# Step 0's last head pair in two halves of two batches, fewer key rows, and a new order of the opening, in a gated linear attention with a feed-forward on one core

## The chip, the cores and the metric

One core of one Trainium2 chip runs the whole kernel. The metric is the time of one execution in microseconds of device time, the median of the runs shown. The engines are called by their names in the profile: PE is TensorE, DVE is VectorE, ACT is ScalarE, POOL is GpSimd, SP is the queue that issues most loads.

## The reference, cut to what matters

```
f = 1 / (1 + exp(-f_logit))                      # batch 4, 8 heads, 768 tokens, 48 channels
for t in range(768):
    state = f[t] * state + k[t] (outer) v[t]     # per batch and head, 48 x 48
    y[t] = q[t] @ state
h = x @ w_in                                     # x: y as 3072 tokens x 384;  w_in 384 x 2048
g = h if h >= 1, 0 if h <= -1, else (h + 1)**2 / 4
out = g @ w_out                                  # 2048 x 384
```

## The kernel before, in words

The 768 tokens are cut into six steps of 128. The eight heads go two by two: four pairs, numbered 0 to 3, each on 2 x 48 partitions, with four batches of 128 tokens side by side (512 columns). Pair 3's rows are split over the three 128-row blocks of x from step 1 on; in step 0 pair 3 stands in rows of its own.

Step 0 is the opening, and it has functions of its own. For each pair `first_loads` loads 192 KB of logits (`raw<-in_l`, for pair 2 `sd<-in_l`) and 512 KB of keys and queries (`kq<-in_k`), and ACT takes the logarithm of the gates in two passes, "log" (L455, L456). `first_gates` sums the logarithms by eight PE matmuls with a triangular mask (L465; each batch is a matmul), takes two exponentials on ACT, "sig" (L468, L469), and multiplies keys and queries by them on DVE, "gate" (L473, L474). `scores` (L572) makes the attention scores of the pair, 16 PE matmuls of 48 rows, and `masks` (L585) multiplies them by the mask on DVE. `last_heads` and `half_tile(own)` (L806) multiply scores by values, `half_tile(not own)` (L836) adds pair 3's result to blocks 0 to 2 of x, and whichever of the two comes first for a block begins its sum; where `own` comes first, a matmul with zeros clears the bank first (L827). The result is split into a high and a low part (L660 on ACT, L661 on DVE), and `unit_0` (L860) begins the feed-forward.

The feed-forward is 96 units, 16 to a step (L266 makes h, nine matmuls of 512 columns; L269, L272, L277 the activation on ACT and DVE; L889 and L280 its high and low part; L287 the product with w_out, nine matmuls). Its weights come as 32 pieces of 384 KB (`raw<-in_w`), and each is split by ACT and DVE (L367, L369, L372, L373) in the first hundred microseconds, while units already run.

The attention of steps 1 to 5 is put between units by hand. `TURNS` says after which unit's in-products pair n (n counts pairs over steps: 4 to 7 are step 1) has its keys turned: on PE for step 1 (L640), on DVE later (L655). `VISITS` gives for pairs n and n+1 the three units at which scores are made (L621), at which the first products with values and the states are made (L688, L759), and at which the outputs follow (L710). The gates of steps 1 to 5 need a scan on DVE (L503), two exponentials on ACT and two products on DVE (L508, L509), and six small moves by SP for pair 3 (`kq<-kq`, L296). `START` is the order in which the opening's work is given to PE, and `WARM` is a row of matmuls on zeros (L337) that PE runs first.

PE runs in the order in which the program gives its work. For DVE, ACT, POOL and SP a planner (`Plan.order`) places each instruction at the time it works out from a table of costs: among those that are ready it takes the one whose latest allowed time, counted back from the end through all that depends on it, is first. Where PE would wait in the plan, it fills the place with matmuls on zeros (L332).

Of the kernel before, what the change touches and what calls it, by code (L numbers as in the profile page):

```python
# [18 lines left out]
AF = mybir.ActivationFunctionType  # L19
ALU = mybir.AluOpType  # L20
PSUM = bass.MemoryType.PSUM

B, H, S, D = 4, 8, 768, 48
C = 128
NI = S // C
NP = H // 2
R = 112
DM, DF = H * D, 2048
NJ = DF // 128
N = B * C  # L30
# [15 lines left out]
NG = (NP + (NI - 1) * NT) * B  # L46


SMALL_PRODUCTS = ("gates", "scores", "heads", "own", "tile", "both", "begin", "before", "part", "states", "parts", "half", "turn")

HOP, LANDING, PER_KB, NEAR, ADDING, PATIENCE, FLAG_BY = 200, 2200, 3.0, 3500, 1500, 0, 60000
COST = dict(gates=870, log=500, mm=227, scores=1100, heads=950, own=1200, tile=680, both=1090, begin=480, before=930, part=560, states=850, parts=830, turn=350, first=110, last=95,
            rows=316, scan=1140, dve=602, small=200, half=490, sums=467, gate=600, act=575, bits=520, join=465, part_hi=440, cast_384=330, cast=400, round=485, copy=520, turned=412, sig=538, decay=226,
            issue=480, near=600, least=300)


TURNS = {4: 4, 5: 5, 6: 9, 7: 9, 8: 19, 9: 19, 10: 25, 11: 25, 12: 28, 13: 28, 14: 37, 15: 37, 16: 40, 17: 40, 18: 47, 19: 47, 20: 61, 21: 61, 22: 70, 23: 70}
VISITS = {4: (5, 6, 7), 6: (10, 12, 13), 8: (21, 22, 25), 10: (25, 26, 28), 12: (28, 32, 37), 14: (37, 39, 40), 16: (40, 46, 47), 18: (47, 60, 61), 20: (61, 69, 70), 22: (70, 75, 77)}
START = (("gates", 3), ("gates", 0), ("scores", 3), ("mask", 3), ("gates", 1), ("scores", 0), ("mask", 0), ("gates", 2), ("last", 3),
         ("scores", 1), ("mask", 1), ("heads", 0), ("scores", 2), ("mask", 2), ("tile", 2), ("tile", 1), ("tile", 0), ("heads", 1), ("heads", 2), ("unit", 0), ("unit", 1), ("unit", 2))  # L60
WARM = 28 * (128,) + 4 * (256,)
BY_PRODUCT, ON_EITHER = (), 16
AFTER = {0: (("turn", 0), ("turn", 1)), 1: (("states", 0),), 2: (("turn", 2), ("turn", 3)), 3: (("states", 2),)}

# [119 lines left out]
def gla_moe(ctx: ExitStack, tc: tile.TileContext, ff, ld, kd, kqd, f0, vv, vl, wd, maskd, identd, gates, values, headsd, out):  # L184
# [50 lines left out]
    def wide(a):  # L235
        return a.rearrange("r b c -> r (b c)")
# [197 lines left out]
    def spread(a):  # L434

        return of_heads(a)[..., 0:D]
# [7 lines left out]
    def first_loads(n):  # L444

        c, a = att[n], LOGS[n]
        if n == NP - 1:
            ready["mask"] = add("ACT", "issue", lambda: nc.scalar.dma_start(mask_z, maskd[:, 0:C + 1]), kb=64)
            ready["sel"] = dma(ident, identd, 64)
        raw_l = WEIGHTS[n][1][:, 0:BOTH]  # L450
        l = dma(raw_l, ld[n], 192)
        rows = 128
        c["lk"] = dma(kq[n][:rows, 0:2 * N], kd[n, :rows], 4 * rows)

        e = sca("log", lambda: nc.scalar.activation(spread(a), raw_l.rearrange("t (m h d) -> t m h d", m=B, h=2), AF.Exp, scale=-1.0), l, cleared)  # L455
        c["l"] = sca("log", lambda: nc.scalar.activation(spread(a), spread(a), AF.Ln, bias=one), e, set_consts)  # L456

    def first_gates(n):

        t, c, (kw, qw) = kq[n][:R], att[n], [a[:R] for a in WEIGHTS[n]]  # L460
        _, ps, held = bank((1, 2, 0, 0)[n])

        def sums():
            for m in range(B):
                nc.tensor.matmul(ps[:R, B - 1 - m], LOGS[n][:, m * C:m * C + R], mask_z[:, 0:C], start=True, stop=True)  # L465

        c["lf"] = o = add("PE", "gates", sums, c["l"], ready["mask"], held)
        k = sca("sig", lambda: nc.scalar.activation(kw, wide(ps)[:R], AF.Exp, scale=-1.0), o)  # L468
        q = c["s2"] = sca("sig", lambda: nc.scalar.activation(qw, wide(ps)[:R, ::-1], AF.Exp), o)  # L469
        held[:] = c["exp"] = [k, q]  # L470
        c["en"] = add("POOL", "least", lambda: nc.gpsimd.tensor_copy(
            out=ok[:R, 1 + n * B:1 + n * B + B], in_=kw.rearrange("r (b c) -> r b c", b=B)[:, ::-1, C - 1]), k)
        c["km"] = vec("gate", lambda: nc.vector.tensor_tensor(out=t[:, 0:N], in0=t[:, 0:N], in1=kw, op=ALU.mult), k, c["lk"])  # L473
        c["qm"] = vec("gate", lambda: nc.vector.tensor_tensor(out=t[:, N:2 * N], in0=t[:, N:2 * N], in1=qw, op=ALU.mult), q, c["lk"])  # L474
        c["kq"] = [c["km"], c["qm"]]

    def first_decays():

        ready["mask_t"] = dma(mask_t, maskd[:, C + 1:], 32)
        o = sca("small", lambda: nc.scalar.activation(f0s, f0s, AF.Exp, scale=-1.0), dma(f0s, f0, 38))  # L480
        o = sca("small", lambda: nc.scalar.activation(f0s, f0s, AF.Ln, bias=one), o, set_consts)
        ready["f0"] = sca("small", lambda: nc.scalar.activation(f0s, f0s, AF.Exp, scale=-1.0), o)
        for n in range(NP):
            f0m = f0s[:R, n * B:n * B + B]
            att[n]["pf"] = add("POOL", "least", lambda f0m=f0m, n=n: nc.gpsimd.tensor_tensor(
                out=f0m, in0=ok[:R, 1 + n * B:1 + n * B + B], in1=f0m, op=ALU.mult), att[n]["en"], ready["f0"])
# [33 lines left out]
    def elementwise(n):  # L520
# [19 lines left out]
        if p == NP - 1:  # L540

            cols = slice(0, 2 * N + B)
            gone = old(n - NP, "sc", "y", "tr", "db")
            c["to"] = []
            for t, m in enumerate(ours):
                o = gates_of[m]
                d = [o["km"], o["qm"], o["pf"][0]]
                o["to"] = [move(kq[NP - 1][z + 16 * t:z + 16 * t + 16, cols], kq[t][r:r + 16, cols], d, set_kq, gone) for r, z in ((48, 0), (112, 64))]
                c["to"] += o["to"]
        c["kq"] = c["to"] if p == NP - 1 else [gates_of[m][a] for m in ours for a in ("km", "qm")]  # L550
        c["db"] = []
# [8 lines left out]
        c["db"].append(sca(B * COST["decay"], decayed, d, state_of[i - 1, p // 2], old(n - 2, "y", "se"), set_ds))  # L560

    lent = {}

    def scores(n):

        c = att[n]
        held = [bank(b) for b in ((5, 6), (3, 4), (5, 2), (3, 4))[n]]

        def emit():
            for m in range(B):  # L570
                for (a, z), (_, ps, _) in zip(HEADS, held):
                    nc.tensor.matmul(ps[:, m], key(n, m)[a:z], query(n, m)[a:z], start=True, stop=True)  # L572

        c["sc"] = add("PE", "scores", emit, c["kq"], [h[2] for h in held])
        c["held"] = held

    am_of = [am[2:4], kn, am[0:2], am[0:2]]

# [573 lines left out]
```

## Time and profile before

| what | value |
|---|---|
| median of 3 runs | 469.62 us (469.57 to 469.84) |
| profiled execution | 469.33 us, its span 467.5 us |
| PE busy | 460.9 us, 99% of the span |
| DVE, ACT busy | 346.5 us (74%), 299.4 us (64%) |

The span runs from the first to the last instruction, and the time of the profiled execution is 1.8 us longer than it. An engine's busy share is a mean over the opening, the hundred microseconds in which weights are split, and a long quiet rest; the share of one of them is read in that stretch alone.

### The profile page before, as it was taken

What the parts mean: (1) busy time and instruction counts of PE and PEld (TensorE: products, weight loads), DVE (VectorE), ACT (ScalarE), POOL (GpSimd) and SP (SyncE); (2) the same over time, 40 slices, a digit from 0 to 9 for tenths busy, and PEclk for the clock granted to TensorE, in tenths of its full rate; (3) what the DMA queues carried; (4) which work ended last, traced back from release to release, by engine and by line L of the source; (5) the groups of instructions that cost most, each with busy time, mean ns of one, the idle gap of its engine ahead of it and who ended that gap; (6) DMA issues with size and microseconds to landing.
All of it is one profiled execution on the core that took longest, in us unless ns stands there. A gap on an engine that the chain in (4) does not pass through costs nothing.

```text
span 467.5 us, 11025 instructions
## 1 busy us (share of the span) xinstructions
PE 460.9 (99%) x4525; PEld 378.8 (81%) x4525; DVE 346.5 (74%) x689; ACT 299.4 (64%) x551; POOL 22.6 (5%) x75
## 2 busy tenths in 40 slices
PE   8999999999999999999999999999999999999996
PEld 7887788888888888888888888888888888888884
DVE  2989998789999889989878788566766755533332
ACT  7798998989566776578475546654545454644443
POOL 2202010000000200000020001000000000000000
PEclk9999999999999999999999999999999999999999
DMA  8878685444023333053335323245322224300001
GB/s 271 310 241 257 187 285 181 169 129 145 1 69 126 105 78 102 2 193 109 75 84 193 129 67 91 68 130 127 126 81 70 67 79 126 102 1 0 1 0 71
DMA packets 21861, 54.36 MB, mean 116 GB/s; under 512 B 3568, under 2 KB 4464, under 8 KB 21808
## 3 DMA queue, kind: packets, MB, share of 16 engines
q1 hardware_dynamic: 21664, 53.57, 37.0%
q8 instruction: 36, 0.59, 0.6%
q14 instruction: 17, 0.14, 0.1%
q10 hardware_dynamic: 144, 0.07, 0.1%
HBM read 44.96 MB, written 4.72 MB: 106 GB/s over the span
## 4 chain that ended last, share of the span: by engine, by line
PE 92%; DVE 3%; ACT 2%; DMA 1%; issue 1%; SPq 0%; DVEq 0%; ACTq 0%
PE po L287 41%; PE ph L266 39%; PE pa L688 2%; PE pa L710 2%; PE ph L621 1%; DVE kn L655 1%; DMA raw<-in_l 1%; PE pa L759 1%; PE po L572 1%; PE pa L806 1%; DVE glo L280 1%; PE pa L640 1%; PE ph L860 0%; DVE act L277 0%; PE pa L621 0%
## 5 line engine op out<-in xcount | busy, mean ns | idle before, releaser
L266 PE MATMUL ph<-x,w_hi 128*128 128x512 f32 x570 | 146.5, 389 | 0.0
L269 ACT ACTIVATE act<-ph,half 128x512 f32<-128x512 f32 x96 | 66.1, 689 | 93.2 <-PE ph L266 92.8
L266 PEld LDWEIGHTS ph<-x,w_hi 128*128 128x128 f32 x570 | 106.8, 188 | 22.6 <-ACT w_hi L372 0.4
L277 DVE SCALAR_TENSOR_TENSOR act<-ph,act 128x512 f32<-128x512 f32 x96 | 66.2, 690 | 61.6 <-ACT act L272 60.5
L889 ACT CAST ghi<-act 128x512 fp32r<-128x512 f32 x96 | 59.4, 619 | 51.1 <-DVE act L277 50.5
L287 PE MATMUL po<-ghi,w_hi 128*128 128x512 f32 x288 | 86.3, 401 | 0.0
L287 PE MATMUL po<-ghi,w_lo 128*128 128x512 f32 x288 | 83.2, 390 | 0.0
L287 PE MATMUL po<-glo,w_hi 128*128 128x512 f32 x288 | 82.9, 389 | 0.0
L280 DVE TENSOR_TENSOR glo<-act,ghi 128x512 fp32r<-128x512 f32 x96 | 66.2, 689 | 21.5 <-ACT ghi L889 20.0
L266 PE MATMUL ph<-x,w_lo 128*128 128x512 f32 x285 | 81.7, 389 | 0.0
L655 DVE STREAM_TRANSPOSE kn<-kq 32x128 f32<-32x128 f32 x224 | 67.7, 302 | 3.6
L287 PEld LDWEIGHTS po<-ghi,w_lo 128*128 128x128 f32 x288 | 54.1, 188 | 11.6
L287 PEld LDWEIGHTS po<-glo,w_hi 128*128 128x128 f32 x288 | 54.1, 188 | 11.5
L266 PEld LDWEIGHTS ph<-x,w_lo 128*128 128x128 f32 x285 | 53.5, 188 | 11.1
L272 ACT ACTIVATE act<-act 128x512 f32<-128x512 f32 x96 | 60.7, 632 | 2.9
L287 PEld LDWEIGHTS po<-ghi,w_hi 128*128 128x128 f32 x288 | 51.9, 188 | 11.3 <-ACT ghi L889 0.3
L383 DVE TENSOR_REDUCE ok<-raw 128x1 f32<-128x384 f32 x64 | 33.2, 545 | 2.2 <-DMA raw<-in_w 2.2
L367 ACT ACTIVATE bits<-raw,top_of 128x384 uint32<-128x384 fp8e4 x32 | 20.1, 642 | 1.1 <-DMA raw<-in_w 1.1
L558 ACT ACTIVATE sd<-sd,kq 112x48 f32<-112x48 f32 x80 | 19.2, 324 | 0.0
L373 DVE TENSOR_TENSOR w_lo<-bits,w_hi 128x384 fp32r<-128x384 f32 x32 | 17.6, 554 | 1.9 <-ACT w_hi L372 1.7
L503 DVE TENSOR_TENSOR_SCAN w<-rec,f 128x512 f32<-128x512 f32 x15 | 18.3, 1220 | 0.9 <-ACT f L502 0.8
L369 DVE SCALAR_TENSOR_TENSOR bits<-raw,bits 128x384 uint32<-128x384 uint32 x32 | 17.4, 550 | 0.0
(137 smaller groups left out, 372.5 us busy)
## 6 DMA issues: line engine op xcount, KB each, us to landing
raw<-in_w SPq DMA_DIRECT2D x32, 384.0 KB, 3.1
raw<-in_w SPq DMA_DIRECT2D x32, 383.6 KB, 3.8
kq<-in_kq SPq DMA_DIRECT2D x15, 512.0 KB, 5.0
v<-in_v SPq DMA_DIRECT2D x12, 384.0 KB, 4.6
out_y<-raw SPq DMA_DIRECT2D x18, 256.0 KB, 2.7
f<-in_f SPq DMA_DIRECT2D x15, 256.5 KB, 3.3
kq<-in_k SPq DMA_DIRECT2D x4, 512.0 KB, 7.2
kq<-kq SPq DMA_DIRECT2D x30, 64.2 KB, 3.5
```

The lines of the kernel that those rows point to most:

```text
L266: nc.tensor.matmul(ps, w_in(w_hi if high else w_lo, j, kt), xt[:, kt, t], start=(n == 0), stop=(n == 8))
L269: nc.scalar.activation(a, ps, AF.Relu, bias=half, scale=0.5)
L272: nc.scalar.activation(a, a, AF.Square)
L277: nc.vector.scalar_tensor_tensor(out=a, in0=ps, scalar=1.0, in1=a, op0=ALU.max, op1=ALU.min)
L280: nc.vector.tensor_tensor(out=lo, in0=a, in1=hi.bitcast(F32), op=ALU.subtract)
L287: nc.tensor.matmul(po[e], w_out(part, j, e), g, start=(j == 0 and n == 0), stop=(j == NJ - 1 and n == 2))
L367: m = sca("bits", lambda: nc.scalar.activation(t, top, AF.Abs, bias=top_of, scale=2.0 ** 30), loaded, made[k - 4] if k >= 4 else None, set ...
L383: seen.append(vec("join", lambda z=z, op=op: nc.vector.tensor_reduce(out=ok[:, 1 + NG + z + c:2 + NG + z + c], in_=words_of(raw[2])[1].bit ...
L503: s1 = vec("scan", lambda: nc.vector.tensor_tensor_scan(out=wide(w), data0=wide(rec), data1=ft[:, N:0:-1], initial=0.0, op0=ALU.mult, op1= ...
L558: nc.scalar.activation(ds[:, at + b * D:at + (b + 1) * D], state[:, p * B + b], AF.Copy, scale=pf[:R, b:b + 1])
L655: nc.vector.transpose(kn[n % 2][to:to + 32, ::-1, r:r + 32], src[:, :, u:u + 32])
L889: o = g["hi"] = sca("copy", lambda: nc.scalar.copy(hi, a), o, unit_out.get(u - 2))
```

## The change

In step 0, pair 3's logits are loaded as two halves of 96 KB, the first by SP and the second by ACT's queue, ahead of the mask. Its logarithms, gate sums, exponentials, products and scores are made for batches 0 and 1 and then for batches 2 and 3: twice as many instructions of half the columns on ACT and DVE, the same matmuls in two groups on PE. `("gates", 7)` and `("scores", 7)` in `START` are the second halves. For all four pairs only the 112 rows of keys and queries that are used are loaded (448 KB instead of 512); the 16 rows of pair 3 that are used later are loaded by a separate 64 KB load, for which the moves into them wait. `START` has a new order: the gates of pairs 2 and 1 and pair 3's heads come ahead of the scores of pair 0, and each block of x begins with pair 3's part, so that nothing is cleared. `TURNS` and `VISITS` move some of the attention of steps 1 to 5 by one to four units, and `WARM` is 7 matmuls of 512 columns and 2 of 256 in place of 28 of 128 and 4 of 256. In the planner's table the halves get costs of their own (not shown in the diff).

```
--- before.py
+++ after.py
@@ -46,19 +46,19 @@
 NG = (NP + (NI - 1) * NT) * B
 
 
 
             rows=316, scan=1140, dve=602, small=200, half=490, sums=467, gate=600, act=575, bits=520, join=465, part_hi=440, cast_384=330, cast=400, round=485, copy=520, turned=412, sig=538, decay=226,
             issue=480, near=600, least=300)
 
 
-TURNS = {4: 4, 5: 5, 6: 9, 7: 9, 8: 19, 9: 19, 10: 25, 11: 25, 12: 28, 13: 28, 14: 37, 15: 37, 16: 40, 17: 40, 18: 47, 19: 47, 20: 61, 21: 61, 22: 70, 23: 70}
-VISITS = {4: (5, 6, 7), 6: (10, 12, 13), 8: (21, 22, 25), 10: (25, 26, 28), 12: (28, 32, 37), 14: (37, 39, 40), 16: (40, 46, 47), 18: (47, 60, 61), 20: (61, 69, 70), 22: (70, 75, 77)}
-START = (("gates", 3), ("gates", 0), ("scores", 3), ("mask", 3), ("gates", 1), ("scores", 0), ("mask", 0), ("gates", 2), ("last", 3),
-         ("scores", 1), ("mask", 1), ("heads", 0), ("scores", 2), ("mask", 2), ("tile", 2), ("tile", 1), ("tile", 0), ("heads", 1), ("heads", 2), ("unit", 0), ("unit", 1), ("unit", 2))
-WARM = 28 * (128,) + 4 * (256,)
+TURNS = {4: 4, 5: 4, 6: 8, 7: 8, 8: 15, 9: 15, 10: 25, 11: 25, 12: 28, 13: 28, 14: 37, 15: 37, 16: 40, 17: 40, 18: 46, 19: 46, 20: 61, 21: 61, 22: 69, 23: 69}
+VISITS = {4: (4, 5, 6), 6: (10, 12, 13), 8: (21, 22, 26), 10: (26, 27, 29), 12: (28, 32, 37), 14: (37, 39, 40), 16: (40, 46, 47), 18: (47, 60, 61), 20: (61, 69, 70), 22: (70, 75, 77)}
+START = (("gates", 3), ("gates", 7), ("gates", 0), ("scores", 3), ("scores", 7), ("mask", 3), ("gates", 2), ("gates", 1), ("last", 3),
+         ("scores", 0), ("scores", 1), ("mask", 0), ("tile", 0), ("heads", 0), ("scores", 2), ("mask", 1), ("tile", 1), ("heads", 1), ("mask", 2), ("tile", 2), ("heads", 2), ("unit", 0), ("unit", 1), ("unit", 2))
+WARM = 7 * (512,) + 2 * (256,)
 BY_PRODUCT, ON_EITHER = (), 16
 AFTER = {0: (("turn", 0), ("turn", 1)), 1: (("states", 0),), 2: (("turn", 2), ("turn", 3)), 3: (("states", 2),)}
 
@@ -444,37 +444,60 @@
     def first_loads(n):
 
         c, a = att[n], LOGS[n]
+        raw_l = WEIGHTS[n][1][:, 0:BOTH]
+        c["l"] = []
+        parts = 2 if n == NP - 1 else 1
+        some = [slice(k * B // parts, (k + 1) * B // parts) for k in range(parts)]
+        loads = []
+        for k in range(parts):
+            cols = slice(k * BOTH // parts, (k + 1) * BOTH // parts)
+            if k == 0:
+                loads.append(dma(raw_l[:, cols], ld[n, :, cols], 192 / parts))
+            else:
+                loads.append(add("ACT", "issue", lambda cols=cols: nc.scalar.dma_start(raw_l[:, cols], ld[n, :, cols]), kb=192 / parts))
         if n == NP - 1:
             ready["mask"] = add("ACT", "issue", lambda: nc.scalar.dma_start(mask_z, maskd[:, 0:C + 1]), kb=64)
             ready["sel"] = dma(ident, identd, 64)
-        raw_l = WEIGHTS[n][1][:, 0:BOTH]
-        l = dma(raw_l, ld[n], 192)
-        rows = 128
-        c["lk"] = dma(kq[n][:rows, 0:2 * N], kd[n, :rows], 4 * rows)
-
-        e = sca("log", lambda: nc.scalar.activation(spread(a), raw_l.rearrange("t (m h d) -> t m h d", m=B, h=2), AF.Exp, scale=-1.0), l, cleared)
-        c["l"] = sca("log", lambda: nc.scalar.activation(spread(a), spread(a), AF.Ln, bias=one), e, set_consts)
+        c["lk"] = dma(kq[n][:R, 0:2 * N], kd[n, :R], 4 * R)
+        log = "log" if parts == 1 else "half_log"
+        for m, l in zip(some, loads):
+            e = sca(log, lambda m=m: nc.scalar.activation(spread(a)[:, m], raw_l.rearrange("t (m h d) -> t m h d", m=B, h=2)[:, m], AF.Exp, scale=-1.0), l, cleared)
+            c["l"].append(sca(log, lambda m=m: nc.scalar.activation(spread(a)[:, m], spread(a)[:, m], AF.Ln, bias=one), e, set_consts))
 
     def first_gates(n):
 
+        k, n = divmod(n, NP)
         t, c, (kw, qw) = kq[n][:R], att[n], [a[:R] for a in WEIGHTS[n]]
-        _, ps, held = bank((1, 2, 0, 0)[n])
+        parts = len(c["l"])
+        if k == 0:
+            c["ps"] = bank((1, 2, 0, 0)[n])
+            c["was"], c["lf"], c["exp"], c["s2"], c["km"], c["qm"], c["kq"] = list(c["ps"][2]), [], [], [], [], [], []
+        _, ps, held = c["ps"]
+        some = range(k * B // parts, (k + 1) * B // parts)
+        back = slice(N - (k + 1) * N // parts, N - k * N // parts)
+        on = slice(k * N // parts, (k + 1) * N // parts)
+        half = "" if parts == 1 else "half_"
 
         def sums():
-            for m in range(B):
+            for m in some:
                 nc.tensor.matmul(ps[:R, B - 1 - m], LOGS[n][:, m * C:m * C + R], mask_z[:, 0:C], start=True, stop=True)
 
-        c["lf"] = o = add("PE", "gates", sums, c["l"], ready["mask"], held)
-        k = sca("sig", lambda: nc.scalar.activation(kw, wide(ps)[:R], AF.Exp, scale=-1.0), o)
-        q = c["s2"] = sca("sig", lambda: nc.scalar.activation(qw, wide(ps)[:R, ::-1], AF.Exp), o)
-        held[:] = c["exp"] = [k, q]
-        c["en"] = add("POOL", "least", lambda: nc.gpsimd.tensor_copy(
-            out=ok[:R, 1 + n * B:1 + n * B + B], in_=kw.rearrange("r (b c) -> r b c", b=B)[:, ::-1, C - 1]), k)
-        c["km"] = vec("gate", lambda: nc.vector.tensor_tensor(out=t[:, 0:N], in0=t[:, 0:N], in1=kw, op=ALU.mult), k, c["lk"])
-        c["qm"] = vec("gate", lambda: nc.vector.tensor_tensor(out=t[:, N:2 * N], in0=t[:, N:2 * N], in1=qw, op=ALU.mult), q, c["lk"])
-        c["kq"] = [c["km"], c["qm"]]
+        c["lf"].append(add("PE", half + "gates", sums, c["l"][k], ready["mask"], c["was"]))
+        o = c["lf"][-1]
+        e = sca(half + "sig", lambda: nc.scalar.activation(kw[:, back], wide(ps)[:R, back], AF.Exp, scale=-1.0), o)
+        q = sca(half + "sig", lambda: nc.scalar.activation(qw[:, on], wide(ps)[:R, ::-1][:, on], AF.Exp), o, c["l"])
+        c["s2"].append(q)
+        c["exp"] += [e, q]
+        held[:] = c["exp"]
+        if k == parts - 1:
+            c["en"] = add("POOL", "least", lambda: nc.gpsimd.tensor_copy(
+                out=ok[:R, 1 + n * B:1 + n * B + B], in_=kw.rearrange("r (b c) -> r b c", b=B)[:, ::-1, C - 1]), c["exp"])
+        c["km"].append(vec(half + "gate", lambda: nc.vector.tensor_tensor(out=t[:, back], in0=t[:, back], in1=kw[:, back], op=ALU.mult), e, c["lk"]))
+        c["qm"].append(vec(half + "gate", lambda: nc.vector.tensor_tensor(out=t[:, N:][:, on], in0=t[:, N:][:, on], in1=qw[:, on], op=ALU.mult), q, c["lk"]))
+        c["kq"] += [c["km"][-1], c["qm"][-1]]
 
     def first_decays():
+        rest_of_keys.append(dma(kq[NP - 1][R:, 0:2 * N], kd[NP - 1, R:], 4 * (128 - R)))
 
         ready["mask_t"] = dma(mask_t, maskd[:, C + 1:], 32)
         o = sca("small", lambda: nc.scalar.activation(f0s, f0s, AF.Exp, scale=-1.0), dma(f0s, f0, 38))
@@ -545,7 +568,7 @@
             for t, m in enumerate(ours):
                 o = gates_of[m]
                 d = [o["km"], o["qm"], o["pf"][0]]
-                o["to"] = [move(kq[NP - 1][z + 16 * t:z + 16 * t + 16, cols], kq[t][r:r + 16, cols], d, set_kq, gone) for r, z in ((48, 0), (112, 64))]
+                o["to"] = [move(kq[NP - 1][z + 16 * t:z + 16 * t + 16, cols], kq[t][r:r + 16, cols], d, rest_of_keys, gone) for r, z in ((48, 0), (112, 64))]
                 c["to"] += o["to"]
         c["kq"] = c["to"] if p == NP - 1 else [gates_of[m][a] for m in ours for a in ("km", "qm")]
         c["db"] = []
@@ -560,19 +583,23 @@
         c["db"].append(sca(B * COST["decay"], decayed, d, state_of[i - 1, p // 2], old(n - 2, "y", "se"), set_ds))
 
     lent = {}
+    rest_of_keys = [set_kq]
 
     def scores(n):
 
+        k, n = divmod(n, NP)
         c = att[n]
-        held = [bank(b) for b in ((5, 6), (3, 4), (5, 2), (3, 4))[n]]
+        parts = len(c["l"])
+        if k == 0:
+            c["held"] = [bank(b) for b in ((5, 6), (3, 4), (5, 2), (3, 4))[n]]
+            c["sc"] = []
 
         def emit():
-            for m in range(B):
-                for (a, z), (_, ps, _) in zip(HEADS, held):
+            for m in range(k * B // parts, (k + 1) * B // parts):
+                for (a, z), (_, ps, _) in zip(HEADS, c["held"]):
                     nc.tensor.matmul(ps[:, m], key(n, m)[a:z], query(n, m)[a:z], start=True, stop=True)
 
-        c["sc"] = add("PE", "scores", emit, c["kq"], [h[2] for h in held])
-        c["held"] = held
+        c["sc"].append(add("PE", "scores" if parts == 1 else "half_scores", emit, c["kq"][2 * k:2 * k + 2] if parts > 1 else c["kq"], [h[2] for h in c["held"]] if k == 0 else []))
 
     am_of = [am[2:4], kn, am[0:2], am[0:2]]
 
```

## Rows read from the trace of the kernel before

**Rows 1.** The page's first part: busy us of each engine and instructions.
```profile
PE 460.9 (99%) x4525; PEld 378.8 (81%) x4525; DVE 346.5 (74%) x689; ACT 299.4 (64%) x551; POOL 22.6 (5%) x75
```

**Rows 2.** The chain that ended last: start us, us, what.
```profile
2.23 5.72 DMA raw<-in_l
...
11.01 0.37 PE po L572
...
15.34 0.32 PE pa L827
...
21.23 2.28 PE ph L860 x9
...
64.34 2.04 PE po L287 x9
```

**Rows 3.** PE in order of time, the opening: start us, us, instruction, count.
```profile
1.07 4.02 PE L337 MATMUL ph<-zeros 128*128 128x128 bf16 x32 [1.07 <-DVE zeros L306]
5.00 1.48 PE L465 MATMUL pa<-mask,act 128*112 128x128 f32 x8
...
8.56 1.16 PE L572 MATMUL po<-kq 48*128 48x128 f32 x16 [0.35 <-DVE kq L474]
9.65 1.13 PE L465 MATMUL pa<-mask,f 128*112 128x128 f32 x8
```

**Rows 4.** Loads issued at 0.84, 1.75, 2.70 and 4.9: KB, us to landing.
```profile
raw<-in_l SPq DMA_DIRECT2D x1, 192.0 KB, 2.8
...
kq<-in_k SPq DMA_DIRECT2D x1, 512.0 KB, 5.3
...
kq<-in_k SPq DMA_DIRECT2D x1, 512.0 KB, 6.8
...
v<-in_v SPq DMA_DIRECT2D x1, 384.0 KB, 8.3
```

**Rows 5.** DVE in order of time, the opening.
```profile
7.19 0.72 DVE L473 TENSOR_TENSOR kq<-kq,raw 112x512 f32<-112x512 f32 x1 [6.17 <-ACT raw L468]
7.83 0.68 DVE L474 TENSOR_TENSOR kq<-kq,raw 112x512 f32<-112x512 f32 x1
9.66 0.69 DVE L473 TENSOR_TENSOR kq<-kq,raw 112x512 f32<-112x512 f32 x1 [1.16 <-ACT raw L468]
...
18.66 0.67 DVE L585 TENSOR_TENSOR am<-pa,mask 128x512 f32<-128x512 f32 x1
19.26 0.54 DVE L373 TENSOR_TENSOR w_lo<-bits,w_hi 128x384 fp32r<-128x384 f32 x1
19.72 0.55 DVE L369 SCALAR_TENSOR_TENSOR bits<-raw,bits 128x384 uint32<-128x384 uint32 x1
```

**Rows 6.** ACT in order of time, pair 3's first exponential.
```profile
6.51 0.60 ACT L468 ACTIVATE raw<-pa 112x512 f32<-112x512 f32 x1 [0.51 <-PE pa L465]
```

**Rows 7.** Busy us in stretches: us, then PE, PEld, DVE, ACT, POOL.
```profile
9.66:21.00 11.34, 11.11 (x137) 9.25 (x135) 11.32 (x20) 8.47 (x17) 3.82 (x12) 1.00 0.96 356
21.00:41.00 20.00, 20.00 (x157) 16.18 (x152) 17.77 (x33) 17.76 (x33) 0.74 (x2) 1.00 0.77 255
```

**Rows 8.** PE in order of time, steps 0 and 1 of the units.
```profile
44.19 0.61 PE L332 MATMUL po<-zeros 128*128 128x512 bf16 x2
...
46.93 0.55 PE L640 MATMUL pa<-ident,kq 112*128 112x112 f32 x4
...
69.32 0.58 PE L640 MATMUL pa<-ident,kq 112*128 112x112 f32 x4 [0.52 <-DVE glo L280]
```

**Rows 9.** DVE in order of time, the gates of pair 5.
```profile
42.45 1.22 DVE L503 TENSOR_TENSOR_SCAN w<-rec,f 128x512 f32<-128x512 f32 x1
...
45.96 0.69 DVE L508 TENSOR_TENSOR kq<-kq,w 128x512 f32<-128x512 f32 x1
```

**Rows 10.** SP's queue in order of time, the moves after pair 6's gates.
```profile
63.23 1.14 SPq L296 DMA_DIRECT2D kq<-kq  x2
```

**Rows 11.** The second of these moves: KB, us to landing.
```profile
kq<-kq SPq DMA_DIRECT2D x1, 64.2 KB, 5.3
```

More of the change, by code (lines that the diff above doesn't have):

```diff
@@ L46 @@
 NG = (NP + (NI - 1) * NT) * B
-SMALL_PRODUCTS = ("gates", "scores", "heads", "own", "tile", "both", "begin", "before", "part", "states", "parts", "half", "turn")
+SMALL_PRODUCTS = ("gates", "scores", "heads", "own", "tile", "both", "begin", "before", "part", "states", "parts", "half", "turn", "half_gates", "half_scores")
 HOP, LANDING, PER_KB, NEAR, ADDING, PATIENCE, FLAG_BY = 200, 2200, 3.0, 3500, 1500, 0, 60000
-COST = dict(gates=870, log=500, mm=227, scores=1100, heads=950, own=1200, tile=680, both=1090, begin=480, before=930, part=560, states=850, parts=830, turn=350, first=110, last=95,
+COST = dict(half_gates=460, half_scores=570, half_log=330, half_sig=330, half_gate=350, gates=870, log=500, mm=227, scores=1100, heads=950, own=1200, tile=680, both=1090, begin=480, before=930, part=560, states=850, parts=830, turn=350, first=110, last=95,
```

## The prediction

> **What bounds the kernel now.** I read the page's busy times first, then the chain that ended last, then PE, DVE and ACT in order of time through the opening, then the loads one by one, and last the stretches. PE is busy 460.9 us of 467.5 [rows 1], so what matters is when it begins to be busy for good and where it waits after that. In the chain the reader is to see that from 11.01 us on everything is PE, one matmul behind the other, down to `unit_0` at 21.23 [rows 2]. From there the end follows at a fixed distance, unless PE waits. So this change is worth what it takes from the time of `unit_0`, less what it adds of waits behind it.
>
> Ahead of 11.01 the opening waits for loads. Pair 3's keys are issued at 1.75 and land 5.3 later, at 7.05 [rows 4]; DVE's first product starts at 7.19, although its row names ACT, whose exponential ended at 7.11 [rows 5, 6]. Both are late at once: to hurry only one of them brings nothing. DVE ends pair 3's products at 8.51, PE starts its scores at 8.56 and the next gates at 9.65 [rows 3, 5].
>
> The second thing to see is that DVE has no room in the opening. Between 9.66 and 21.00 it is busy 11.32 of 11.34 us; from 21 to 41 it idles 2.23 of 20 [rows 7]. PE is the bound by a small margin only.
>
> **The change part by part.** [...]
>
> *Logits in halves:* the whole load lands 2.8 us after its issue [rows 4]. A half lands no later than that unless the two queues disturb each other; the mask goes one issue later on ACT's queue. The exponentials follow the sums, and the whole one ends at 7.11 today; four of half the size must be through by about 7. At nothing, at worst 0.3 (half an exponential of 0.60 [rows 6]).
>
> *112 rows:* 64 KB less for each pair. From 7.05 to 13.2, when the second load of v lands [rows 4], 2,176 KB arrive, 0.35 MB per us, so 64 KB is 0.18 us. The halves add 128 short packets ahead of the keys. I take a landing at 6.95, between 6.87 and 7.05. The later 64 KB load lies behind all of these, and the first move that needs it comes with step 1.
>
> *Products and scores in halves:* DVE's instructions start 0.60 apart at 512 columns and 0.46 apart at 384 [rows 5], so 256 columns cost 0.32, and a pair of halves 0.04 more than the whole. First half: 6.95 + 0.32 + 0.41 = 7.68, so PE's scores start at 7.75 instead of 8.56. The second half ends at 8.32, and PE, which needs 0.55 for its first half, has it at 8.37: done by 8.95 instead of 9.65.
>
> [...]
>
> *The new order:* PE's work from the scores of pair 3 to `unit_0` is 1.09 + 1.04 (8.56 to 9.65, and the next gates) + 10.22 (11.01 to 21.23) = 12.35 us. No bank is cleared any more: less 0.32 [rows 2]. From 7.75, with 12.03 us and a wait of 0.07, `unit_0` would start at 19.85, a gain of 1.38: the upper bound. DVE gives the lower one. It starts 0.24 sooner, loses 0.08 to the splits, and idles from 8.32 to the masks of pair 3 at about 9.0 instead of 1.15 before 9.66 [rows 5]: 0.5 less. So its work, and with it the masks ahead of the last heads, is through 0.66 sooner, or only 0.2 sooner if it waits again, say because pair 0's keys are now behind other loads. I take 0.9 for the opening, between 0.2 and 1.4. Pair 3's heads now come ahead of the scores of pair 0, so whatever makes them late (masks, v, ACT's work on pair 0's bank) stands in front of all of these on PE.
>
> *Places, steps 1 and 2:* pair 5 is turned after unit 4 instead of 5, and its scores are made there too; today PE reaches them at 46.93, and the key product has ended 0.28 earlier, at 45.96 + 0.69 = 46.65 [rows 8, 9]. They are now wanted about 5.5 us sooner. A scan and two products (1.22 + 2 x 0.6 = 2.4 us) must go ahead of weight pieces on DVE. The bounds are nothing (it idles 2.23 of these 20 us) and 2.4 (nothing else gives way). I take 0.4, near the lower end, because units 5 and later then come later by the inserted scores and the weights have that long. Queued behind on PE: all units. In return the two zero matmuls that the plan put at 44.19 should go: 0.45, and none if the plan finds another gap.
>
> Pair 7 is turned after unit 8 instead of 9. Today that turn waits 0.52 until 69.32 [rows 8]. The row names DVE, but the last move was issued at about 63.8 and landed 5.3 later, at 69.1 [rows 10, 11]: it waited for the move. After unit 8 PE is there some 4 us sooner (64.34 [rows 2], then the four matmuls of pair 6's turn). So the gates of pair 6 must be made 4 to 5 us sooner on DVE. I leave the wait at its 0.5: at nothing, between -0.5 and +1.
>
> One visit at unit 4 saves a change from long to short matmuls, one at unit 27 to 29 adds one: nothing. Pairs 8, 18 and 22 are turned earlier on DVE alone, far from the bound: nothing, but 8 and 9 now lie within the last weight pieces.
>
> Sum: -0.9 - 0.45 + 0.4 = -0.95. The profiled execution is 469.33 (span 467.5 and 1.8 around it), the median 469.62, 0.29 more. 469.62 - 0.95 = 468.7.
>
> **The rivals.** *No new waits:* gates come in time at units 4 and 8, and the wait of 0.52 goes. For it: DVE's idle time up to 41, and gates need no load that is late. Against: DVE is nearly full. -0.9 - 0.45 - 0.5 = -1.85: 467.8; with 1.4 in the opening 467.3.
>
> *The gain is swallowed:* DVE is the bound already, in the opening and up to unit 10. `unit_0` starts 0.4 sooner, the pairs of step 1 cost 0.8 of waits, the 0.45 is saved: 469.6. For it: 11.32 of 11.34 us [rows 7], gates that end 0.28 ahead of use. This is also how it goes if halves do nothing because keys and not sums decide: then scores start at 8.4 and only the zero matmul and the idle time are won.
>
> *Slower:* the move into pair 7's rows is not brought forward. PE would come to that turn at about 63.4 and find the move landing at 69.1, with the out-products of unit 7 and the in-products of unit 9 still ahead, nine matmuls or 2.04 each [rows 2], which today lie before it: 4 us later than now, 473.6 at the worst. It decides from a landing at about 65.9, where the loss reaches 0.9; a move issued 2 us sooner than today gives 471.6.
>
> **How the numbers follow.** The forecast, 468.2 to 469.2, has 0.38; no new waits 0.30; swallowed 0.18; slower 0.14. A measurement of this kernel tells about 0.2% from no change, 0.94 us, so the line lies at 468.7, in the middle of the forecast: half of it counts as faster. Faster 0.19 + 0.30, about 0.5; same 0.19 + 0.18, about 0.36; slower 0.14. The range goes from 467.3 (the largest gain in the opening without new waits) to 470.2: the swallowed case with a wait of half a microsecond more. It leaves out most of the slower case and little below. The forecast's own range is 468.2 to 469.2.
>
> **What would show it.** In the profile after: keys of pair 3 landing at 6.9 to 7.0 and the first 8 scores at 7.7 to 7.9; no L827; `unit_0` at 20.0 to 20.7; DVE still without idle time up to there; no L332 near unit 4 and 5; the turn of pair 5 with a wait of some tenths ahead of it; pair 7's turn behind the landing of its moves. [...]

## The result and the profile after

The changed kernel takes 474.26 us (median of 9 runs, 471.26 to 475.73), the kernel before 469.62 (9 runs, 468.69 to 470.44). The ratio is 1.0094, with a 95% interval of 1.0070 to 1.0118: slower by 0.9%, where 468.7 was forecast, with a chance of about 0.5 of being faster and 0.14 of being slower. The profiled execution is the slowest of the nine, 475.73 us with a span of 473.9; its rows show where the time went, and its sizes are a little above those of the median.

The page's first part of the changed kernel, which answers to [rows 1]:

```profile
PE 462.2 (98%) x4495; PEld 377.7 (80%) x4495; DVE 346.0 (73%) x690; ACT 299.4 (63%) x556; POOL 22.5 (5%) x75
```

PE has 30 matmuls fewer and is busy 1.3 us longer, but the span is 6.4 us longer: PE waited more. The loads one by one, issued at 1.76, 3.18, 3.65 and 4.12 (KB, us to landing), for [rows 4]:

```profile
kq<-in_k SPq DMA_DIRECT2D x1, 448.0 KB, 6.3
...
kq<-in_k SPq DMA_DIRECT2D x1, 448.0 KB, 8.8
...
v<-in_v SPq DMA_DIRECT2D x1, 384.0 KB, 10.3
...
kq<-in_k SPq DMA_DIRECT2D x1, 448.0 KB, 11.8
```

Pair 3's keys are an eighth smaller and land at 8.06, one us later than the whole 512 KB did; the third pair's keys land at 15.9. The stretches, for [rows 7] (after the granted clock, the last two columns are the busy share of the DMA engines and GB/s):

```profile
9.66:21.00 11.34, 8.66 (x107) 7.25 (x107) 7.61 (x13) 6.31 (x14) 2.88 (x11) 1.00 1.05 266
21.00:41.00 20.00, 19.81 (x154) 14.76 (x152) 16.86 (x31) 17.53 (x34) 0.36 (x4) 1.00 0.73 243
```

The DMA engines are as busy as before (1.05 against 0.96) and move 266 GB/s instead of 356. DVE, which was full, now idles 3.7 of 11.34 us. DVE and PE in order of time through the opening, for [rows 5] and [rows 3]:

```profile
8.12 0.42 DVE L495 TENSOR_TENSOR kq<-kq,raw 112x256 f32<-112x256 f32 x1 [7.11 <-ACT raw L488]
...
10.72 1.29 DVE L612 TENSOR_TENSOR am<-po,mask 128x512 f32<-128x512 f32 x2 [1.17 <-PE po L600]
...
15.98 0.69 DVE L495 TENSOR_TENSOR kq<-kq,raw 112x512 f32<-112x512 f32 x1 [2.63 <-DMA kq<-in_k]
```

```profile
6.23 1.20 PE L483 MATMUL pa<-mask,act 128*112 128x128 f32 x4 [0.58 <-ACT act L465]
7.22 1.91 PE L483 MATMUL pa<-mask,f 128*112 128x128 f32 x8
9.06 1.63 PE L600 MATMUL po<-kq 48*128 48x128 f32 x16
...
14.04 1.08 PE L833 MATMUL pa<-am,v 128*48 128x128 f32 x16 [1.42 <-DMA v<-in_v]
...
17.34 1.16 PE L600 MATMUL po<-kq 48*128 48x128 f32 x16 [1.12 <-DVE kq L496]
...
24.78 0.50 PE L887 MATMUL ph<-x,w_lo 128*128 128x512 f32 x1
```

The reader is to see one chain: the first scores at 9.06 (8.56 before), pair 3's heads waiting 1.42 us for v, DVE waiting 2.63 us for keys, the next scores waiting for DVE, and `unit_0` at 24.78 instead of 21.16 (21.23 in the chain of [rows 2]). The eight gate products at 7.22 take 0.24 us each, nearly twice what eight of them take at 10.62 (1.13 us, 0.14 each). The granted clock of that stretch reads 1.00, but this trace's record of it begins only at 10.07 us, so whether a lower clock did that is not settled. It costs nothing on this chain: behind these matmuls PE stands idle for v and DVE for the keys, and both of these loads had been issued by 4.12.

For the units behind the opening, here are the starts of some units' in-products (PE in order of time), as us sooner (-) or later than in the kernel before. The last column is the time from the landing of the last output, when the DMA goes idle, to the end of the span.

| kernel | unit 1 | unit 10 | unit 25 | unit 30 | unit 47 | unit 95 | ending |
|---|---|---|---|---|---|---|---|
| before (start; ending) | 24.05 | 71.82 | 140.46 | 167.76 | 247.21 | 454.63 | 2.0 |
| changed | +4.44 | +3.66 | +3.66 | +4.05 | +4.69 | +4.72 | 3.4 |
| all rows (e1) | -0.08 | -1.77 | -1.77 | -1.38 | -0.71 | -0.70 | 1.9 |
| all rows, later load (e12) | -0.49 | -1.66 | -1.66 | -1.28 | -0.66 | -0.66 | 3.5 |
| 112 rows alone (e2) | +2.04 | +1.15 | +1.15 | +1.14 | +1.13 | +1.15 | 2.1 |
| new, then old places (e7) | +0.06 | -1.69 | -1.69 | -1.70 | -1.68 | -1.62 | 1.8 |

Three things are in it: some 4.5 us lost in the opening, 0.8 won back up to unit 10 with 1.0 given away by unit 47, and 1.4 us more at the very end, where no work of the kernel is left.

### The profile page after: what moved, and what is told of

Its sections match the earlier page's. It is cut to its first block, busy times and chain, and to the rows that moved or that the text cites. A ratio compares the mean times of both kernels' runs of the same rounds, so it can differ in the third digit from the quotient of the medians.

```text
span 473.9 us, 10963 instructions
## 1 busy us (share of the span) xinstructions
PE 462.2 (98%) x4495; PEld 377.7 (80%) x4495; DVE 346.0 (73%) x690; ACT 299.4 (63%) x556; POOL 22.5 (5%) x75
## 3 DMA queue, kind: packets, MB, share of 16 engines
HBM read 44.76 MB, written 4.72 MB: 104 GB/s over the span
## 5 line engine op out<-in xcount | busy, mean ns | idle before, releaser
L266 PEld LDWEIGHTS ph<-x,w_lo 128*128 128x128 f32 x285 | 53.5, 188 | 11.1
L287 PEld LDWEIGHTS po<-ghi,w_hi 128*128 128x128 f32 x288 | 51.9, 188 | 11.1 <-ACT ghi L916 0.3
L530 POOL COPY end<-w 128x4 f32<-128x4 f32 x15 | 5.5, 368 | 261.1 <-ACT w L529 261.1
```

Source lines behind the costliest of these rows:

```text
L266: nc.tensor.matmul(ps, w_in(w_hi if high else w_lo, j, kt), xt[:, kt, t], start=(n == 0), stop=(n == 8))
L287: nc.tensor.matmul(po[e], w_out(part, j, e), g, start=(j == 0 and n == 0), stop=(j == NJ - 1 and n == 2))
```

## The experiments

### All rows again

```diff
-        c["lk"] = dma(kq[n][:R, 0:2 * N], kd[n, :R], 4 * R)
+        c["lk"] = dma(kq[n][:, 0:2 * N], kd[n], 512)
-        rest_of_keys.append(dma(kq[NP - 1][R:, 0:2 * N], kd[NP - 1, R:], 4 * (128 - R)))
```

> The changed kernel, but with all 128 rows of keys loaded for every pair (512 KB instead of 448, no later load of 16 rows). Theory (loads of 112 rows run at about half the rate): the loads move about 400 GB/s between 8 and 18 us again, as before the change, instead of 186 to 260; the opening's first in-products come near 20.5 us instead of 24.8, and the time is 467.5 to 469.5. Rival A (the short packets of the half logits, or the order of the loads, slow the queue): the rate stays at 200 to 260 GB/s and the time near 474. Rival B (PE's low clock and the new order of PE's work lose the time, not the loads): the rate returns, but the time stays above 472.

Measured: 469.26 us, ratio 0.9996 (0.9983 to 1.0009). The whole loss goes. The windows from 8 to 14 us of the kernel before, the changed one and this one (at the end DMA share and GB/s):

```profile
8.00:14.00 6.00, 5.42 (x65) 4.62 (x64) 4.84 (x9) 4.82 (x10) 0.97 (x3) 1.00 1.04 400
8.00:14.00 6.00, 4.62 (x38) 4.04 (x36) 4.01 (x8) 4.88 (x11) 1.01 (x3) 1.00 1.05 217
8.00:14.00 6.00, 5.72 (x70) 5.00 (x72) 5.12 (x10) 5.38 (x11) 2.27 (x7) 1.00 1.04 405
```

The rate is back, and DVE is as busy again as before the change (9.65 of 13 us from 5 to 18; before 9.64, changed 6.04). So Rivals A and B are out: the half logits, the order of the loads and PE's new order are still in this kernel. With halves, new order and full loads unit 1 comes only 0.08 us sooner.

### All rows, with the later load kept

This kernel has the changed kernel's instructions on PE, DVE, ACT and SP, and the later load brings the same 16 rows a second time: what differs from the changed kernel is the size of four loads, and from the kernel above one 64 KB load.

```diff
-        c["lk"] = dma(kq[n][:R, 0:2 * N], kd[n, :R], 4 * R)
+        c["lk"] = dma(kq[n][:, 0:2 * N], kd[n], 512)
-        rest_of_keys.append(dma(kq[NP - 1][R:, 0:2 * N], kd[NP - 1, R:], 4 * (128 - R)))
+        rest_of_keys.append(dma(kq[NP - 1][R:, 0:2 * N], kd[NP - 1, R:], 4 * (128 - R), att[NP - 1]["lk"]))
```

> The changed kernel with 128 rows of keys loaded for every pair, and the later 64 KB load of pair 3's last 16 rows kept (it loads the same rows a second time). Its instructions are as many as the changed kernel's on PE, DVE and ACT, and only the size of four loads differs. If the 112 rows are the whole loss of the changed kernel, it runs like the kernel with all rows and no later load (469.26): 469.0 to 469.6. If a part of the loss is the late piece of code, 8 KB, that the changed kernel and the one with 112 rows for pair 3 load 2.2 us behind the last output and that the others don't have, then it comes back here: the same units, but a span that ends 3.5 us behind the last output instead of 2.0, and about 470.7. If the later load itself hurts, unit 1 comes later than 24.0.

Measured: 471.12 us, ratio 1.0042 (1.0027 to 1.0057). The units of the table are sooner than before by 0.5 to 1.7 us, and still the time is longer than without the later load, by 1.9 us between the medians (0.46% between the ratios). The windows of its end, from the landing of the last output on:

```profile
465.25:467.25 2.00, 0.00 (x0) 0.00 (x0) 0.00 (x0) 0.00 (x0) 0.00 (x0) 0.90 0.00 0
467.25:467.50 0.25, 0.00 (x0) 0.00 (x0) 0.00 (x0) 0.00 (x0) 0.00 (x0) 0.50 0.09 33
467.50:468.70 1.20, 0.00 (x0) 0.00 (x0) 0.00 (x0) 0.00 (x0) 0.00 (x0) 0.50 0.00 0
```

Two us after the outputs something moves 33 GB/s for a quarter of a us, 8 KB, and the program ends 1.2 us behind it. The changed kernel does the same; its windows, and the row of its instruction queue from 460 us on, which has 4 packets where the kernel before and the one with all rows have 3:

```profile
470.50:472.50 2.00, 0.00 (x0) 0.00 (x0) 0.00 (x0) 0.00 (x0) 0.00 (x0) 0.59 0.00 0
472.50:472.75 0.25, 0.00 (x0) 0.00 (x0) 0.00 (x0) 0.00 (x0) 0.00 (x0) 0.50 0.10 33
472.75:473.90 1.15, 0.00 (x0) 0.00 (x0) 0.00 (x0) 0.00 (x0) 0.00 (x0) 0.50 0.00 0
```

```profile
q14 instruction: 4, 0.03, 0.5%
```

So the fourth packet is, by its queue, a piece of program, loaded when all work is done. The expectation's second case holds: the late piece is a part of the loss, and not the whole.

### The later load on ACT's queue

```diff
-        rest_of_keys.append(dma(kq[NP - 1][R:, 0:2 * N], kd[NP - 1, R:], 4 * (128 - R)))
+        rest_of_keys.append(add("ACT", "issue", lambda: nc.scalar.dma_start(kq[NP - 1][R:, 0:2 * N], kd[NP - 1, R:]), att[0]["l"], kb=4 * (128 - R)))
```

> The changed kernel with the later 64 KB load issued on ACT's queue instead of SP's, so that SP has one issue less, as in the kernels without the late piece of code. If that piece belongs to SP's program, it goes, and the time falls by about 1.4 us, to 472.9, with loads as slow as in the changed kernel (180 to 260 GB/s) and unit 1 still at about 28.5. If the piece belongs to another engine or to the ending, 474.3 and the late load stays.

Measured: 473.65 us (6 runs, 472.07 to 474.19), ratio 1.0088 (1.0068 to 1.0107). The windows of its end:

```profile
467.25:469.50 2.25, 0.00 (x0) 0.00 (x0) 0.00 (x0) 0.50 (x1) 0.00 (x0) 1.00 0.93 357
469.50:471.90 2.40, 0.00 (x0) 0.00 (x0) 0.00 (x0) 0.00 (x0) 0.00 (x0) 0.53 0.00 0
```

The late piece is gone, and the ending is 2.4 us: in this kernel it goes with the one issue on SP's queue. The time fell by 0.6 us and not by 1.4, within what the runs scatter, so the size is not confirmed here. The loss of the 112 rows stays: from 5 to 18 us 258 GB/s, unit 1 later by 3.72. In this profile the granted clock is 0.87 in that stretch, but the clock does not make the loss: of the six runs, the one with a granted clock of 1.000 over the whole span took 473.94 us, and one with 0.991 took 473.49.

### The rows alone, on the kernel before

```diff
-        c["lk"] = dma(kq[n][:rows, 0:2 * N], kd[n, :rows], 4 * rows)
+        c["lk"] = dma(kq[n][:R, 0:2 * N], kd[n, :R], 4 * R)
...
+        rest_of_keys.append(dma(kq[NP - 1][R:, 0:2 * N], kd[NP - 1, R:], 4 * (128 - R)))
```

> The kernel before with one edit: 112 rows of keys are loaded, and the 16 rows of pair 3 later. Theory: the rate falls to about 220 GB/s between 5 and 18 us, unit 0 starts 3 to 4 us later than 21.2, and the time is 472 to 474. Rivals A and B: the rate stays near 400 GB/s, the keys land a little sooner, and the time is 469 to 470.

Measured: 471.41 us, ratio 1.0053 (1.0033 to 1.0073). With whole logits and the old order pair 3's keys land at about 7.1, as before; the later loads lose, 300 GB/s from 8 to 14 us, and unit 1 comes 2.04 later. So the rows alone make the kernel slower, as the theory has it, but by about half of the size that it gave. This kernel has the additional issue on SP too, but not the late piece of code (ending 2.1). So the issue does not bring that piece by itself; what else decides it was not tested.

### 112 rows for pair 3 alone

```diff
-        c["lk"] = dma(kq[n][:R, 0:2 * N], kd[n, :R], 4 * R)
+        rows = R if n == NP - 1 else 128
+        c["lk"] = dma(kq[n][:rows, 0:2 * N], kd[n, :rows], 4 * rows)
```

> The changed kernel with 112 rows loaded for pair 3 alone (and its 16 rows later), 128 for pairs 0 to 2. With 128 for all the time was 469.3, with 112 for all 474.3. Theory (each load of 112 rows slows the queue while it runs): about a quarter of the 5 us, 470 to 471, and the rate back at 400 GB/s from about 8 us on. [...]

Measured: 471.50 us, ratio 1.0055 (1.0036 to 1.0075), the same as with all rows and the later load (1.0042), within the intervals. That lies above the 470 to 471 that was expected, which did not know of the late piece. Its loads are back at 380 GB/s, unit 1 is 0.42 sooner, and the ending has the late piece (3.5 us). One short load among whole ones costs little and brings nothing; the loss comes with the three that follow it, for which the number of rows is the only difference from the changed kernel.

### Loads by themselves

Two kernels that only load keys, eight loads of one kind after the other, and compute nothing of the reference.

```python
STAGES = (("whole", ((0, 128),), 1024), ("rows_112", ((0, 112),), 1024), ("short_rows", ((0, 128),), 896), ("rows_96", ((0, 96),), 1024),
          ("64_and_48", ((0, 64), (64, 112)), 1024), ("96_and_16", ((0, 96), (96, 112)), 1024), ("rows_64", ((0, 64),), 1024), ("again", ((0, 128),), 1024))
```

> Only loads, nothing of the reference is computed: eight loads of keys in a row by SP, and all landed before the next stage, in eight stages: 128 rows of 4 KB; 112 rows; 128 rows of 3.5 KB (the bytes of 112 rows); 96 rows; 112 rows as 64 and 48; 112 rows as 96 and 16; 64 rows; 128 rows again. Theory (it is the 112 rows that are slow by themselves): 128 rows near 400 GB/s, the short rows near 380, 112 rows at 190 to 260. [...] Rival: 112 rows alone run at the rate of 128, and the opening is slow for another reason.

The windows inside its stages, in that order (after the clock, DMA share and GB/s; one execution):

```profile
5.00:14.00 9.00, 3.79 (x5) 0.00 (x0) 1.00 0.95 357
19.00:30.00 11.00, 0.00 (x0) 0.00 (x0) 1.00 1.03 274
34.00:42.50 8.50, 0.00 (x0) 0.00 (x0) 1.00 1.01 394
46.50:56.50 10.00, 0.00 (x0) 0.00 (x0) 1.00 1.02 283
60.00:76.00 16.00, 0.00 (x0) 0.00 (x0) 1.00 1.03 221
80.00:94.00 14.00, 0.00 (x0) 0.00 (x0) 1.00 1.03 254
98.50:108.00 9.50, 0.00 (x0) 0.00 (x0) 1.00 0.99 209
112.00:122.00 10.00, 0.00 (x0) 0.00 (x0) 1.00 0.98 360
```

With the DMA engines busy all the time, 112 rows move 274 GB/s where 128 rows move 357 to 360. As many bytes taken off the length of the rows instead (128 rows of 3.5 KB) lose nothing: 394. So the rival is out, and so is a rule by the count of rows alone, since 96 rows are not slower than 112 (283). To cut the 112 rows into two loads is worse, 221 and 254.

The second kernel asks which rows: 0 to 127, 16 to 127, 0 to 111, 0 to 119, 0 to 103, 64 to 127, 0 to 31, 0 to 127.

> Loads alone, eight of one kind after the other, nothing of the reference computed. Rows 0 to 127 again (357 GB/s before), rows 16 to 127, rows 0 to 111 (274 before), 120 rows, 104 rows, rows 64 to 127, 32 rows, rows 0 to 127. If the rate goes by which partitions are reached, so that what lacks is the share of some of them, rows 16 to 127 run as 112 rows did, 120 rows take no longer than 128 rows (335 GB/s or more) and 104 rows lie between 96 and 112 (about 280). If it goes by how the count of rows divides among the 16 DMA engines, 104 and 120 rows, which leave half an engine's round, are slower than 112, and rows 16 to 127 are as rows 0 to 111. If the first rows matter, rows 16 to 127 differ from rows 0 to 111.

DVE's reads at the end of each stage; the idle time in front is what the eight loads took (the first stage also lies behind memsets):

```profile
32.51 0.58 DVE L68 COPY seen<-t 128x1 f32<-128x1 f32 x8 [16.40 <-DMA t<-in_k]
47.80 0.58 DVE L68 COPY seen<-t 128x1 f32<-128x1 f32 x8 [14.71 <-DMA t<-in_k]
67.23 0.58 DVE L68 COPY seen<-t 128x1 f32<-128x1 f32 x8 [18.85 <-DMA t<-in_k]
86.08 0.58 DVE L68 COPY seen<-t 128x1 f32<-128x1 f32 x8 [18.27 <-DMA t<-in_k]
99.09 0.58 DVE L68 COPY seen<-t 128x1 f32<-128x1 f32 x8 [12.43 <-DMA t<-in_k]
106.31 0.58 DVE L68 COPY seen<-t 128x1 f32<-128x1 f32 x8 [6.64 <-DMA t<-in_k]
121.23 0.58 DVE L68 COPY seen<-t 128x1 f32<-128x1 f32 x8 [14.35 <-DMA t<-in_k]
```

Eight whole loads take 14.35 us. Eight of 112 rows take 14.71 (rows 0 to 111) or 16.40 (rows 16 to 127), of 120 rows 18.85, of 104 rows 18.27: less data and more time. Only 64 rows (12.43) and 32 rows (6.64) are quicker. In the first kernel, by bytes and the rates above, an estimate without the beginning of a stage and its last landing, eight whole loads take 11.7 us, 112 rows 13.4, 96 rows 11.1 and rows of 3.5 KB 9.3. Two of its windows, inside the stages of 120 and of 104 rows:

```profile
54.00:64.00 10.00, 0.00 (x0) 0.00 (x0) 1.00 0.96 232
70.00:83.00 13.00, 0.00 (x0) 0.00 (x0) 1.00 0.83 208
```

Here the engines' busy share is down to 0.96 and 0.83, which is 0.93 and 0.81 of the 1.03 with 112 rows. With 112 rows the engines are as busy as with whole loads (1.03 against 0.95 and 0.98 in the first kernel), and yet they move 274 GB/s instead of 357 to 360.

None of the three expectations holds alone. By the partitions reached, 120 rows should have run at 335 GB/s or more. By the division among engines, 104 and 120 rows are slower (208 and 232 GB/s against 253 and 295), as they should be, but it does not say why 112 rows are slow, and how a load's rows fall to the engines no run shows. Rows 16 to 127 run at 253 GB/s and rows 0 to 111 at 295, but the first kernel had 274 for those same rows, so whether the place of the rows counts is not settled. Why 112 rows are slow remains open.

### Halves and order with the old places

```diff
+START = (("gates", 3), ("gates", 7), ("gates", 0), ("scores", 3), ("scores", 7), ("mask", 3), ("gates", 1), ("scores", 0), ("mask", 0), ("gates", 2), ("last", 3), ...
```

(128 rows, and `WARM`, `TURNS`, `VISITS` and the rest of `START` as before.)

> The halves alone: all 128 rows are loaded, and the places, the warming matmuls and the order of the opening are those before the change, with the second halves put in behind the first. Theory: the loads are as fast as before the change, pair 3's scores start 0.4 to 0.8 us sooner than 8.56, and the time is 468.8 to 469.6, since DVE is full behind them. [...]

Measured: 476.02 us, ratio 1.0146 (1.0131 to 1.0161). Unit 1 is where it was (-0.04), but the time is outside the expected range. With these tables the plan puts in 20 zero matmuls instead of 6, and units 25 to 95 come later by 0.2 to 5.8; 4.2 of that arises at the four places with zero matmuls from 149 us on. It tells nothing about halves but their -0.04.

```diff
-TURNS = {4: 4, 5: 4, 6: 8, 7: 8, 8: 15, 9: 15, ..., 18: 46, 19: 46, ..., 22: 69, 23: 69}
-VISITS = {4: (4, 5, 6), ..., 8: (21, 22, 26), 10: (26, 27, 29), ...}
+TURNS = {4: 4, 5: 5, 6: 9, 7: 9, 8: 19, 9: 19, ..., 18: 47, 19: 47, ..., 22: 70, 23: 70}
+VISITS = {4: (5, 6, 7), ..., 8: (21, 22, 25), 10: (25, 26, 28), ...}
```

That is the kernel with all rows and the new order, with all places as before.

> The changed kernel with all 128 rows loaded and with TURNS and VISITS as before the change; halves, warming and the order of the opening stay new. In the same kernel with the new places unit 1 started 0.1 us sooner than before and unit 10 started 1.8 us sooner. Theory (the places after units 4 to 10 gave these 1.7 us, not the opening): unit 1 within 0.3 us of 24.05, unit 10 at 71.5 or later, the time 469.3 to 471. Rival (the new order of the opening leaves DVE ahead and so removes the waits): unit 10 near 70.1 and the time 467.5 to 468.7.

Measured: 469.35 us, ratio 0.9998 (0.9986 to 1.0010); unit 1 is 0.17 sooner, unit 10 0.33 and units 30 to 95 0.06. That is the theory: without the new places the 1.8 us at unit 10 do not come.

### The old warm-up

```diff
-WARM = 7 * (512,) + 2 * (256,)
+WARM = 28 * (128,) + 4 * (256,)
```

> All rows loaded, new order, halves and places, but the warm-up matmuls of before (28 of 128 columns and 4 of 256 instead of 7 of 512 and 2 of 256). If the shorter warm-up is worth what it ends sooner, this loses up to 0.4 us: 469.7. If keys decide behind it, 469.3, no difference to the kernel with the new warm-up.

Measured, on the kernel with all rows: 469.15 us, ratio 0.9998 (0.9987 to 1.0009). No difference, as for keys that decide behind it.

### The places apart

The kernel before, with nothing changed but the places of pairs 4 to 7:

```diff
-TURNS = {4: 4, 5: 5, 6: 9, 7: 9, ...
+TURNS = {4: 4, 5: 4, 6: 8, 7: 8, ...
-VISITS = {4: (5, 6, 7), ...
+VISITS = {4: (4, 5, 6), ...
```

> The kernel before with one edit: pairs 4 to 7 at the new places (turned after units 4 and 8, visits of pair 4 after units 4, 5 and 6). Theory (these places are worth 1.7 us by themselves): unit 10 near 70.2 instead of 71.8, the time 467.6 to 468.5. Rival (they only go with the new opening; the planner answers with zero matmuls or waits, as it did with the halves alone): 469.3 to 472.

Measured: 468.78 us, ratio 0.9987 (0.9976 to 0.9997). Unit 10 is 1.61 sooner, as the theory has it, and unit 95 keeps it (-1.59). The time does not: it lies between the two ranges, 0.1% below the kernel before, and the profiled span is only 0.5 us shorter (467.0 instead of 467.5). About 1 us is lost behind the start of unit 95; to what was not found.

The other way round, all rows, new order and the places of pairs 8 and later as before:

> The changed kernel with all 128 rows loaded, and the places of pairs 8 and on as before the change; those of pairs 4 to 7 stay new. With all places new, 1.77 us were won up to unit 25 and 1.07 of these were given back at units 27 to 47. Theory (the later places give them back): the end 1.5 to 1.9 us sooner than before, 467.5 to 468.2. Rival (the loss at units 27 to 47 comes from waits that are there anyway once PE is sooner): 468.6 to 469.4, as with the new places.

Measured: 468.44 us, ratio 0.9981 (0.9970 to 0.9993), the quickest of all: unit 95 is 1.62 sooner, and of that 0.9 us show in the span (466.6). With the new later places unit 95 is 0.70 sooner. The difference lies at two spots: 0.4 between units 25 and 30, where the visits at 26, 27 and 29 make one more, and 0.7 at unit 46, where pair 18 is turned earlier. PE's waits from 20 us on in the changed kernel show a part of the second (engine, line, for what: us, times, longest):

```profile
PE pa L667 <- DVE bits L369: 0.8, 1, 0.8
PE ph L786 <- DVE kn L682: 0.4, 1, 0.4
PE ph L887 <- ACT x L687: 0.2, 1, 0.2
```

The second row is not in the kernel with the old later places: the turned keys (`kn`) are late by 0.4 us for the state products of unit 46. The first is the turn of pair 7, and in the changed kernel it is longer than the 0.52 of [rows 8].

## Why the prediction was wrong

**The step that failed is "112 rows".** It took 64 KB less as 0.18 us less, bytes divided by the 0.35 MB per us of whole loads, with a landing at 6.95 and bounds of 6.87 and 7.05. Pair 3's keys landed at 8.06, and the loads behind them were later still, the next keys at 12.0 instead of 9.5. By themselves loads of 112 rows run at 274 GB/s instead of 357. At equal instructions (changed kernel against all rows with the later load) it costs 1.0094 - 1.0042 of 469.6, 2.4 us; without the late code (later load on ACT against all rows) 1.0088 - 0.9996, 4.3 us; in the old order 2.0 at unit 1. The first two do not agree, so the cost of the rows is known only as 2.4 to 4.3 us, and that of the late code as 0.6 to 1.9. The new order goes with a dearer loss: pair 3's heads, which wait 1.42 us for v, stand there ahead of pair 0's scores. The prediction named that queue and not its price, since it had no late load in it. A bound on the other side was missing: the trace of before had no load of 112 rows, and the price was taken from a rate with no lower end.

**A second cost was in no step: the later load's issue.** "The later 64 KB load lies behind all of these" is right for the data. But with its issue on SP the program loads 8 KB behind the last output: the ending grew from 2.0 to 3.4 us, and the time with all rows by 1.9 us.

**The opening, forecast -0.9, is over-sized even with full loads.** In the five kernels with all rows and the new order unit 1 comes between 0.49 us sooner and 0.06 later. DVE's first product and the beginning of `unit_0`, with the later load and with all rows alone:

```profile
7.05 0.43 DVE L495 TENSOR_TENSOR kq<-kq,raw 112x256 f32<-112x256 f32 x1 [6.04 <-ACT raw L488]
20.65 0.50 PE L887 MATMUL ph<-x,w_lo 128*128 128x512 f32 x1
```

```profile
7.47 0.43 DVE L495 TENSOR_TENSOR kq<-kq,raw 112x256 f32<-112x256 f32 x1 [6.45 <-ACT raw L487]
21.08 0.50 PE L886 MATMUL ph<-x,w_lo 128*128 128x512 f32 x1
```

From the one to the other it is 13.6 us in both, and in the three others too; before the change it is 14.0. The forecast had 6.95 and 20.33, 13.4 us. So behind the first product the forecast is only 0.2 too good. The rest is the landing: whole keys, and with them the first product, come at 7.05 to 7.59 in these five kernels, not at 6.95; why they scatter was not found. That the distance is the same each time fits the rival "the gain is swallowed", in which DVE has no room: it was full in [rows 7]. The logits at nothing held in the changed kernel too, where pair 3's first exponential ended at 7.84, ahead of the keys. The new warm-up brought nothing: with all rows the ratio is 0.9998 with the old one and 0.9996 with the new.

The halves start 0.34 apart, four in 1.36 us where two whole ones take 1.22 at the 0.61 between those of the changed kernel: 0.14 for the split, where the rows of before gave 0.08.

**The places of pairs 4 to 7 were under-sized.** Forecast: -0.45 for the zero matmuls, +0.4 for a wait at unit 4, pair 7's at its 0.5. Measured: 1.6 us sooner by unit 10, in the kernel with these places alone. The zero matmuls go (0.53), no wait shows at unit 4, and between units 4 and 8 about as much again is saved by the visit at unit 4, which the sum had at nothing. The split turn of pairs 6 and 7 with its wait goes too (0.7). PE in order of time in the changed kernel, for [rows 8], has the in-products that begin at 43.86 directly behind the unit before, and the turns of pairs 4 and 5 as one group with no idle time ahead:

```profile
43.86 1.52 PE L266 MATMUL ph<-x,w_hi 128*128 128x512 f32 x6
45.22 0.85 PE L266 MATMUL ph<-x,w_lo 128*128 128x512 f32 x3
45.91 0.93 PE L667 MATMUL pa<-ident,kq 112*128 112x112 f32 x8
```

**The later places, "nothing", cost 1.07**: one more visit is 0.4, not 0, and the earlier turn at unit 46 costs 0.7, of which 0.4 is PE's wait for DVE. It was not "far from the bound".

**The third rival had the right sign for another reason**, and that its 473.6 lies near the time measured is luck. No move into pair 7's rows was late by microseconds: with all rows it is issued at 58.5 instead of 63.8, and in the changed kernel the turn waits 0.8.

The sum at the start of unit 95, from the profile with all rows: -1.7 by the early places, +1.07 by the later ones and nothing by the opening, -0.7 in all. The median with all rows (469.26) does not show it clear of the noise. The 112 rows and the late code then take it to 474.26.

## What to carry to other kernels

Price a load by its shape, not its bytes: if the trace has no load with that number of rows, the price is not bounded, and a kernel of loads alone gives it in one run. For loads like these, shorten rows (3.5 KB: 394 GB/s where whole loads have 357 to 360) rather than drop 16 of 128 (274). When a schedule's places are moved together, read the start of each unit against the kernel before: gains and losses of separate spots then come apart, here -1.7 and +1.07. Then compare the spans too: a gain at the last unit need not reach the end, as with the old later places (1.62 us at unit 95, 0.9 in the span).

## What was not expected of the hardware

Eight loads of 112 rows of 4 KB take 14.7 to 16.4 us, where eight of 128 rows take 14.35, at a full busy share of the DMA engines (1.03). And a single issue more on SP's queue can bring a last load of 8 KB of code after the last output, which makes the program's ending 3.4 to 3.5 us instead of 1.8 to 2.4; in one kernel with the same issue (2.1) it did not.
